# Expert pairs fed by a 128-byte gather and a 32x32 transpose on VectorE

## The chip, the cores and the metric

One core of one Trainium2 chip runs the whole program; there is no work on the other cores and no collective. The metric is the device time of one execution in microseconds. Times come as the median of several executions; the profile is of one execution, whose own time is given beside its span.

## The reference

Three layers follow one another over 4608 tokens (8 batches of 576) with 512 features, all in float32.

```
attn: phi(x) = [exp(p - max|p|), exp(-(p - max|p|))],  p = x @ w_phi
      kv = phi(k)^T v;  out = phi(q) kv / (phi(q) . sum(phi(k)) + 1e-6)      # 8 heads of 64
moe:  logits = x @ w_gate + bias[modality];  e = argmax(logits), gate = softmax(logits)[e]
      out = gate * (relu(x @ w1[e]) @ w2[e])                                  # 8 experts, 512 -> 1024 -> 512
moe2: h = x @ w_in;  s = h * softmax(h);  out = (layernorm(s) * g_ln) @ w_out # 512 -> 1024 -> 512
```

A token goes to one expert only, and which one is known only on the chip. So the middle layer must sort token rows by expert.

## The kernel before

**Attention and gating.** Eight pairs of batch and head group are worked through in 9 steps each. When a pair of batches has its last head group done, `gating` finds each token's expert, its gate and its place. GpSimd (POOL) then sends each tile of 128 token rows with one indirect DMA (line 628) into the DRAM table `xe`, whose rows have 520 floats: 512 features, the gate, the token number, and padding. There are 36 such tiles; those of the last pair of batches (4, 3 and 2 tiles) come at the end of the stage. POOL also adds up the key features (line 322).

**The experts' units.** The tokens of an expert are cut into units: unit 0 (128 rows) and unit 1 (256 rows) of the fullest expert, which start early; 16 pairs of 256 rows (units 2 to 17); one single of 128 rows (unit 18); a "quad" of four small rests; and extras under a condition that is tested once at run time (line 1412). A table in SBUF, worked out by small VectorE instructions in `slot_table` at the end of attention, tells SyncE (SP) where each unit's rows lie; SP reads four of its numbers for each unit (`slot_regs`).

**A unit's rows.** `load_x` (line 913) brings the rows of a unit into the tile `xin` with one DMA, token in the partition, and `keep_gates` (line 922) copies gate and token number from `xe` to another DRAM table. `xT` (line 898) turns the rows on TensorE in squares of 128 by 128 against the identity, eight for a pair and four for the single, into PSUM. `evac` then makes the two float32r parts of the turned rows: ScalarE copies the high part `xTh` (line 887) and VectorE subtracts it from the original for the low part `xTl` (line 888), each in pieces of 128x512. `xTh` and `xTl` have one buffer each, so they may be written for unit u+1 only when the matmuls of `mm1(u)` have read them for unit u.

**A unit's matmuls.** `mm1` (four chunks of w1) and `mm2` (four chunks of w2) run 24 matmuls for each chunk, three for each product of high and low parts (line 1074). Weight chunks are split the same way four chunks ahead (lines 925 and 926): ScalarE the high part, VectorE, or POOL in a few places (`POOL_FIRST = (1, 3)` for unit 1), the low part. Between the chunks of units 2 to 13, `prep` runs the last layer's weight conversion on VectorE in small steps (lines 997 to 1016). In `unit(u)`, after chunk `XAT` of `mm1(u)`, `next_x(u)` is called: `xT(u+1)`, `slot_regs(u+3)`, `load_x(u+2)`. From unit 14 on, blocks of the last layer run between `mm1` and `mm2`.

**What sets the order.** In attention TensorE's order is written out by hand and the other engines' orders come from the planner. From unit 2 to unit 12 the order of all engines is that of the program text; SP's queue is in program order in all of the expert stage. From unit 13 on the planner orders the compute engines of the units again. Each engine works its own queue in order, and so does SP with its DMAs.

Of the kernel before, what the change touches and what calls it, by code (L numbers as in the profile page):

```python
# [8 lines left out]
F32 = mybir.dt.float32  # L9
# [8 lines left out]
P = 128  # L18
B, H, S, D, F = 8, 8, 576, 64, 128
NTOK = B * S  # L20
DM = H * D
E = 8
# [10 lines left out]
PAD = 2 * P  # L33
CAP = NTOK + PAD
ROW = 520
YCOLS = PAD + NTOK
LAG = 8
LAGF = 2
# [152 lines left out]
    return compute  # L191


def attention(ctx, tc, c, cnt, xe, q, k, v, ld, early, m, late):
    nc = tc.nc
    V, A, G, T, SP = nc.vector, nc.scalar, nc.gpsimd, nc.tensor, nc.sync
    ldr = ctx.enter_context(tc.tile_pool(name="a_ldr", bufs=2))
# [371 lines left out]
    def gating(u, first, n):  # L569
        tiles = range(first, first + n)  # L570
        t0 = 9 * u.p2 + first
        gt = gs[0][:, 0:n] if first == 0 else gs[1][:, first - 4 : first - 4 + n]
        w = lambda nm, sh=[P, 5, E], dt=F32: gp.tile(sh, dt, name="g_" + nm)
        L = w("L")[:, :n, :]
        V.tensor_reduce(out=L, in_=gt.rearrange("p t h e -> p t e h"), axis=AX.X, op=ALU.add)
        V.tensor_tensor(out=L, in0=L, in1=c.bias[:, t0 : t0 + n, :], op=ALU.add)
        mx = w("mx", [P, 5])[:, :n]
        V.tensor_reduce(out=mx, in_=L, axis=AX.X, op=ALU.max)
        V.tensor_tensor(out=L, in0=L, in1=mx.unsqueeze(2).broadcast_to([P, n, E]), op=ALU.subtract)
        ex = w("ex")[:, :n, :]  # L580
        A.activation(ex, L, AF.Exp)
        first = w("first")[:, :n, :]
        V.scalar_tensor_tensor(
            out=first, in0=L, scalar=0.0, in1=c.rev.unsqueeze(1).broadcast_to([P, n, E]),
            op0=ALU.is_ge, op1=ALU.mult,
        )
        V.tensor_reduce(out=mx, in_=first, axis=AX.X, op=ALU.max)
        oh = w("oh", dt=BF16)[:, :n, :]
        V.tensor_tensor(
            out=oh, in0=c.rev.unsqueeze(1).broadcast_to([P, n, E]),  # L590
            in1=mx.unsqueeze(2).broadcast_to([P, n, E]), op=ALU.is_equal,
        )
# [12 lines left out]
        V.tensor_reduce(out=sm, in_=ex, axis=AX.X, op=ALU.add)
        V.tensor_scalar(out=sm, in0=sm, scalar1=1e-9, scalar2=None, op0=ALU.add)
        V.reciprocal(sm, sm)
        for part, lo, hi in ((0, 0, 4), (2, 4, 5), (1, 5, 9)):
            i0, i1 = max(lo, tiles[0]), min(hi, tiles[0] + n)
            if i0 < i1:  # L610
                G.tensor_copy(
                    xs[part][:, i0 - lo : i1 - lo, DM : DM + 1], sm[:, i0 - tiles[0] : i1 - tiles[0]].unsqueeze(2)
                )
        yield "0", 1
        base = w("base", [P, 6, E])
        V.tensor_copy(base[:, 0, :], cnt[0])
        for a in range(n):
            V.tensor_tensor(out=base[:, a + 1, :], in0=rk[:, 1, a, :], in1=base[:, a, :], op=ALU.add)
        cnt[0] = base[:, n, :]
        rkb = w("rkb")[:, :n, :]  # L620
        V.tensor_tensor(out=rkb, in0=rk[:, 0], in1=base[:, :n, :], op=ALU.add)
        V.tensor_tensor(out=rkb, in0=rkb, in1=oh, op=ALU.mult)
        dst = w("dst", [P, 5])[:, :n]
        V.tensor_reduce(out=dst, in_=rkb, axis=AX.X, op=ALU.add)
        dsti = w("dsti", [P, 5], I32)
        V.tensor_copy(dsti[:, :n], dst)
        for a, i in enumerate(tiles):
            ins = G.indirect_dma_start(
                out=xe, out_offset=bass.IndirectOffsetOnAxis(ap=dsti[:, a : a + 1], axis=0),
                in_=xt[i], in_offset=None,  # L630
            )
            tc.declare_no_dep(ins.ins, group="scat", reason="rows of distinct tokens are distinct")
            tc.add_to_no_dep_group("scat", ins.ins)

    units = [(p2, g) for p2 in range(B // 2) for g in range(2)]
    mixed = [[("k", i), ("q", i)] for i in range(9)]
# [30 lines left out]
        return U.get(len(units) - 1)  # L667

    unit(0)
    zero = w1p.tile([P, ROW], F32, name="zero")  # L670
    G.memset(zero, 0.0)
    for e in range(E):
        SP.dma_start(
            out=xe[e * CAP : e * CAP + PAD, :].rearrange("(t p) w -> p t w", p=P),
            in_=zero.unsqueeze(1).broadcast_to([P, 2, ROW]),
        )
    hl = {0: s0(*[unit(0), steps[0][1]])}
    n = len(steps)
    feats = {}
# [178 lines left out]


class Moe:  # L860
    def __init__(self, tc, c, early, ld, cv, xtp, xe, yd, gd, w1, w2, w_in, w_out, g_ln, out):
        self.tc, self.c, self.early, self.ld, self.xin, self.cv, self.xtp = tc, c, early, ld, None, cv, xtp
        self.xe, self.yd, self.gd, self.w1, self.w2, self.out = xe, yd, gd, w1, w2, out
        self.w_in, self.w_out, self.g_ln = w_in, w_out, g_ln
        self.regs, self.xs, self.raw, self.chunks, self.nsplit, self.xt = {}, {}, [], {}, 0, {}
# [24 lines left out]
    def xT(self, pool, u):  # L890
        n = self.size(u)
        hi = self.xtp.tile([P, 4, 2 * P], F32R, name="xTh")
        lo = self.xtp.tile([P, 4, 2 * P], F32R, name="xTl")
        x = self.xs.pop(u)
        for t in range(n):
            tp = pool.tile([P, 4, P], F32, name="tp")
            for k in range(4):
                self.tc.nc.tensor.transpose(tp[:, k, :], x[:, t, k * P : (k + 1) * P], self.c.ident)  # L898
            sl = slice(t * P, (t + 1) * P)
            self.evac(hi[:, :, sl], lo[:, :, sl], tp)  # L900
        self.xt[u] = (hi, lo)

    def load_x(self, u):
        SP = self.tc.nc.sync
        n = self.size(u)
        rows = self.xe[bass.ds(self.regs[u][1], n * P), :]
        if u == 0:
            t = self.hr[:, DM:].unsqueeze(1)
            self.x0 = self.hr[:, DM:]
        else:  # L910
            t = self.xin.tile([P, 2, DM], F32, name="xin") if u > 1 else self.raw[7].rearrange("p (t d) -> p t d", t=2)
            self.xs[u] = t
        SP.dma_start(out=t[:, 0:n, :], in_=rows[:, 0:DM].rearrange("(t p) w -> p t w", p=P))
        self.keep_gates(u)

    def cols(self, u):
# [1 line left out]
        return bass.ds(y0, n) if u > 1 else slice(y0, y0 + n)  # L918

    def keep_gates(self, u):  # L920
        rows = self.xe[bass.ds(self.regs[u][1], self.width(u)), :]
        self.tc.nc.sync.dma_start(out=self.gd[self.cols(u), :], in_=rows[:, DM : DM + 2])

    def split(self, src, hi, lo, eng):
        self.tc.nc.scalar.copy(hi, src)
# [538 lines left out]
        block()  # L1464


XAT = 1
ENDMAN = True
START = 14
NMAN = START - 1  # L1470
# [8 lines left out]
@with_exitstack  # L1479
def linear_attention_moe_solu(  # L1480
    ctx, tc, q, k, v, w_phi, modality_id, w_gate, modality_bias, w1, w2, w_in, w_out, g_ln, out
):
    nc = tc.nc
    xe = tc.dram_tile([E * CAP, ROW], F32, name="xe")
    yd = tc.dram_tile([DM, YCOLS], F32, name="yd")
    gd = tc.dram_tile([YCOLS, 2], F32, name="gd")
    cp = ctx.enter_context(tc.tile_pool(name="consts", bufs=1))
    fin = cp.tile([P, E], F32, name="fin")
    ld = ctx.enter_context(tc.tile_pool(name="ld", bufs=3))
    cv = ctx.enter_context(tc.tile_pool(name="cv", bufs=2))  # L1490
    xtp = ctx.enter_context(tc.tile_pool(name="xtp", bufs=1))
    with ExitStack() as c2:
        ca = c2.enter_context(tc.tile_pool(name="a_consts", bufs=1))
        c = setup_consts(nc, cp, ca, w_phi, w_gate)
        cnt = [c.rbase]
        early = Early(nc, cp, c)
        m = Moe(tc, c, early, ld, cv, xtp, xe, yd, gd, w1, w2, w_in, w_out, g_ln, out)
        attention(c2, tc, c, cnt, xe, q, k, v, ld, early, m, lambda: setup_bias(nc, c, ca, modality_id, modality_bias))
        nc.vector.tensor_copy(fin, cnt[0])
    m.tab = slot_table(ctx, tc, c, fin, early)  # L1500
    moe(ctx, m)
# [31 lines left out]
```

## Time and profile before

| | us |
|---|---|
| median of 3 executions (range) | 1341.18 (1339.69 to 1342.89) |
| the profiled execution's own time | 1338.16 |
| its span, first to last instruction | 1336.4 |

| engine | busy, us | share | instructions |
|---|---|---|---|
| TensorE matmul (PE) | 1301.7 | 97% | 9522 |
| VectorE (DVE) | 808.6 | 61% | 1571 |
| ScalarE (ACT) | 666.8 | 50% | 1254 |
| GpSimd (POOL) | 433.1 | 32% | 493 |

The busy share is an average over unlike stages: attention takes the first 437 us, the pairs run from 485 to about 935 us, the rest is the last layer. The mean granted clock of TensorE is 0.991 of full speed. Times in the rows below are microseconds from the span's start unless marked otherwise.

### The profile page before, as it was taken

To read this page: it belongs to the slowest core of one execution; us is meant where nothing else is said; L and a number is where in the kernel's file an instruction comes from. 1 tells how busy PE (TensorE), PEld (TensorE's weight loads), DVE (VectorE), ACT (ScalarE), POOL (GpSimd) and SP (SyncE) were. 2 spreads that over 40 slices of the span, in tenths; PEclk is the share of its full clock that TensorE was granted. 3 is DMA by queue.
4 is the path that set the end of the run, shared out by engine and by line. 5 is a ranking of instruction groups with operands and counts; after the bars stand their busy time and mean duration, and the time that the engine had idled before them with its cause. 6 is when DMAs were issued, how large, how long until landed. Compare 5 with 4: busy or idle time off the path is not lost.

```text
span 1336.4 us, 25467 instructions
## 1 busy us (share of the span) xinstructions
PE 1301.7 (97%) x9522; PEld 1095.8 (82%) x9522; DVE 808.6 (61%) x1571; ACT 666.8 (50%) x1254; POOL 433.1 (32%) x493
## 2 busy tenths in 40 slices
PE   8999999999988989999999999999999999999997
PEld 6676777777765889999999999898987777888885
DVE  8756766866954938888888754444433433444442
ACT  6665766666664335555555654444433343343332
POOL 6646664764763300000000323232323222322331
PEclk9998999999999989999999999999999999999998
DMA  8712321331132132223522212124334542111110
GB/s 238 206 52 88 112 88 56 112 120 48 60 117 71 66 94 72 83 72 106 187 73 72 66 47 64 40 56 150 112 87 150 174 129 85 48 40 48 40 41 24
DMA packets 123119, 120.08 MB, mean 90 GB/s; under 512 B 35664, under 2 KB 109552, under 8 KB 122992
## 3 DMA queue, kind: packets, MB, share of 16 engines
q1 hardware_dynamic: 117008, 99.30, 25.1%
q0 software_dynamic: 5824, 19.04, 3.9%
q8 instruction: 77, 1.26, 0.4%
q14 instruction: 50, 0.41, 0.1%
q10 hardware_dynamic: 160, 0.07, 0.0%
HBM read 148.32 MB, written 33.02 MB: 136 GB/s over the span
## 4 chain that ended last, share of the span: by engine, by line
PE 62%; issue 1%; ACT 0%; POOL 0%; POOLq 0%
PE tp L1074 42%; PE h L1074 15%; PE tp L1098 2%; PE tp L898 1%; PE tp L1349 1%; PE tp L1333 1%; PE tp L1280 0%; POOLq L1529 0%; ACT sq L1253 0%; ACT lnTh L887 0%; PE tp L1109 0%; ACT wab L1268 0%; POOL rs L1258 0%; PE tp L1162 0%; POOL rs L1256 0%
## 5 line engine op out<-in xcount | busy, mean ns | idle before, releaser
L322 POOL TENSOR_TENSOR es<-es,e 128x512 f32<-128x512 f32 x128 | 163.2, 1280 | 102.0 <-ACT e L278 96.2
L1074 PE MATMUL tp<-xTh,whi 128*128 128x256 f32 x432 | 122.5, 284 | 2.3 <-PEq L1412 2.3
L1074 PE MATMUL tp<-xTh,wlo 128*128 128x256 f32 x432 | 121.5, 281 | 1.2 <-DVE wlo L926 1.2
L1233 DVE TENSOR_REDUCE s_mx<-h 128x1 f32<-128x512 f32 x72 | 46.4, 686 | 125.3 <-PE h L1074 125.3
L1074 PE MATMUL tp<-xTl,whi 128*128 128x256 f32 x432 | 121.3, 281 | 0.0
L1074 PE MATMUL tp<-hTl,whi 128*128 128x256 f32 x432 | 120.7, 280 | 0.0
L1074 PE MATMUL tp<-hTh,wlo 128*128 128x256 f32 x432 | 120.7, 279 | 0.0
L1074 PE MATMUL tp<-hTh,whi 128*128 128x256 f32 x432 | 120.5, 279 | 0.0
L926 POOL TENSOR_TENSOR wlo<-ldk,whi 128x1024 fp32r<-128x1024 f32 x6 | 14.6, 2432 | 314.2 <-PE tp L1074 295.5
L271 DVE TENSOR_REDUCE m<-mm 128x4 f32<-128x512 f32 x144 | 97.1, 682 | 23.7 <-PE mm L269 23.0
L1238 ACT ACTIVATE ex<-h,s_mx,gt 128x1024 f32<-128x1024 f32 x36 | 43.4, 1207 | 135.7 <-DVE s_mx L1235 72.2
L1269 POOL DMA_INDIRECT out_dram<-wab,gt x36 | 38.6, 1071 | 221.6 <-ACT wab L1268 220.9
L259 DVE TENSOR_TENSOR lo<-tp,hi 128x512 fp32r<-128x512 f32 x72 | 49.5, 688 | 78.7 <-ACT hi L258 78.5
L267 PE MATMUL mm<-wphi_hi,hi 128*128 128x256 f32 x288 | 94.0, 327 | 1.6 <-ACT hi L258 1.6
L1074 PEld LDWEIGHTS tp<-xTh,whi 128*128 128x128 f32 x432 | 82.0, 190 | 2.8 <-ACTq L1412 2.5
L1074 PEld LDWEIGHTS tp<-xTh,wlo 128*128 128x128 f32 x432 | 81.9, 190 | 1.5 <-DVE wlo L926 1.5
L888 DVE TENSOR_TENSOR lnTl<-tp,lnTh 128x512 fp32r<-128x512 f32 x74 | 47.6, 686 | 58.2 <-ACT lnTh L887 58.2
L338 ACT ACTIVATE qp<-tp 128x512 f32<-128x512 f32 x128 | 69.5, 597 | 25.8 <-PE tp L330 23.0
L1074 PEld LDWEIGHTS tp<-xTl,whi 128*128 128x128 f32 x432 | 82.0, 190 | 0.2
L1074 PEld LDWEIGHTS tp<-hTh,whi 128*128 128x128 f32 x432 | 81.3, 188 | 0.4
L1074 PEld LDWEIGHTS tp<-hTl,whi 128*128 128x128 f32 x432 | 81.2, 188 | 0.3 <-DVE hTl L1089 0.2
L268 PE MATMUL mm<-wphi_lo,hi 128*128 128x256 f32 x288 | 81.5, 283 | 0.0
(427 smaller groups left out, 3930.7 us busy)
## 6 DMA issues: line engine op xcount, KB each, us to landing
ldk<-in_moe_w_dram SPq DMA_DIRECT2D x66, 512.0 KB
ldv<-in_moe_w_dram SPq DMA_DIRECT2D x66, 512.0 KB
ldq<-in_moe_w_dram SPq DMA_DIRECT2D x44, 512.0 KB
yd<-yo SPq DMA_DIRECT2D x36, 256.0 KB
yin<-yd SPq DMA_DIRECT2D x18, 512.0 KB
xin<-xe SPq DMA_DIRECT2D x16, 512.0 KB
ldk<-in_k_dram SPq DMA_DIRECT2D x15, 512.0 KB
ldq<-in_q_dram SPq DMA_DIRECT2D x15, 512.0 KB
```

Source lines behind the costliest of these rows:

```text
L259: V.tensor_tensor(out=lo, in0=tp, in1=hi.bitcast(F32), op=ALU.subtract)
L267: T.matmul(o, lhsT=hi[:, 2 * a + j, :], rhs=c.wphi_hi, start=(j == 0), stop=False, skip_group_check=True)
L268: T.matmul(o, lhsT=hi[:, 2 * a + j, :], rhs=c.wphi_lo, start=False, stop=False, skip_group_check=True)
L271: V.tensor_reduce(out=m, in_=pj, axis=AX.X, op=ALU.max, apply_absolute_value=True)
L322: G.tensor_tensor(out=eo, in0=eo, in1=ev[:, :, r, :], op=ALU.add)
L338: A.activation(u.qp[half][:, fh, 2 * hp : 2 * hp + 2, o : o + 2 * P], tp.rearrange("p (h r) t -> p h (r t)", r=2), AF.Exp, scale=sc,)
L888: self.tc.nc.vector.tensor_tensor(out=lo, in0=tp, in1=hi.bitcast(F32), op=ALU.subtract)
L1074: T.matmul(o, lhsT=l, rhs=r, start=first and n == 0, stop=last and n == 2, skip_group_check=True)
L1098: T.transpose(tp[:, j, :], src[:, (b0 + j) * P : (b0 + j + 1) * P], c.ident)
L1233: V.tensor_reduce(out=mx, in_=h[:, sl], axis=AX.X, op=ALU.max, negate=True)
L1238: A.activation(ex, h, AF.Exp, bias=mx, scale=g, accum_out=sm)
L1269: ins = G.indirect_dma_start(out=out, out_offset=bass.IndirectOffsetOnAxis(ap=ys.pop(i)[2].bitcast(I32), axis=0), in_=ob, in_offset=None,)
```

## The change

The row in DRAM is cut in two tables: `xe` with 512 features a row, and `xg` with 8 floats a row for gate, token number and padding. Each tile of tokens is sent with two indirect DMAs, and the regions in front of each expert's rows are cleared in both tables.

For units 2 and up, `load_x` reads the rows in runs of 32 floats (128 bytes) with four DMAs, one for each group of 32 partitions, so that feature block and token block have changed places and only the 32x32 squares are left to be turned. `xT` then turns all squares of the unit with one VectorE instruction in place, and `split` makes the high part (ScalarE, line 925 of before) and the low part (VectorE, line 926) from SBUF in one piece of 128x1024 each. Units 0 and 1 keep the old way. `XAT` goes from 1 to 3, so that `next_x` comes after the last chunk of `mm1`.

```diff
+GROW = ROW - 512
@@ gating
-            ins = G.indirect_dma_start(
-                out=xe, out_offset=bass.IndirectOffsetOnAxis(ap=dsti[:, a : a + 1], axis=0),
-                in_=xt[i], in_offset=None,
-            )
+            for n, (dst, src) in enumerate(((xe, xt[i][:, 0:DM]), (xg, xt[i][:, DM:ROW]))):
+                ins = G.indirect_dma_start(
+                    out=dst, out_offset=bass.IndirectOffsetOnAxis(ap=dsti[:, a : a + 1], axis=0),
+                    in_=src, in_offset=None,
+                )
@@ attention
     for e in range(E):
-        SP.dma_start(
-            out=xe[e * CAP : e * CAP + PAD, :].rearrange("(t p) w -> p t w", p=P),
-            in_=zero.unsqueeze(1).broadcast_to([P, 2, ROW]),
-        )
+        for dst, w in ((xe, DM), (xg, GROW)):
+            SP.dma_start(
+                out=dst[e * CAP : e * CAP + PAD, :].rearrange("(t p) w -> p t w", p=P),
+                in_=zero[:, 0:w].unsqueeze(1).broadcast_to([P, 2, w]),
+            )
@@ Moe.xT
         x = self.xs.pop(u)
+        if u > 1:
+            hi, lo = [t.rearrange("p k w -> p (k w)")[:, 0 : n * DM] for t in (hi, lo)]
+            self.tc.nc.vector.transpose(x, x)
+            self.split(x, hi, lo, self.tc.nc.vector)
+            self.xt[u] = [t.rearrange("p (k w) -> p k w", k=4) for t in (hi, lo)]
+            return
@@ Moe.load_x
+        elif u > 1:
+            t = self.xin.tile([P, 2 * DM], F32, name="xin")[:, 0 : n * DM]
+            self.xs[u] = t
+            src = rows.rearrange("(t c) (k g r) -> g c k t r", c=32, g=4, r=32)
+            for g in range(4):
+                SP.dma_start(
+                    out=t[32 * g : 32 * g + 32].rearrange("c (k t r) -> c k t r", k=4, r=32), in_=src[g]
+                )
+            self.keep_gates(u)
+            return
@@ Moe.keep_gates
-        rows = self.xe[bass.ds(self.regs[u][1], self.width(u)), :]
-        self.tc.nc.sync.dma_start(out=self.gd[self.cols(u), :], in_=rows[:, DM : DM + 2])
+        rows = self.xg[bass.ds(self.regs[u][1], self.width(u)), :]
+        self.tc.nc.sync.dma_start(out=self.gd[self.cols(u), :], in_=rows[:, 0:2])
@@
-XAT = 1
+XAT = 3
```

## Rows read from the trace of the kernel before

**Rows 1.** Page, part 5: line engine operation, count | busy, mean ns | idle, releaser.

```profile
L322 POOL TENSOR_TENSOR es<-es,e 128x512 f32<-128x512 f32 x128 | 163.2, 1280 | 102.0 <-ACT e L278 96.2
```

**Rows 2.** Chain of waits, one pair unit: start us, us, what.

```profile
586.72 0.87 PE tp L898 x8
587.59 22.49 PE tp L1074 x192
...
```

**Rows 3.** Chain of waits, last units.

```profile
...
874.62 0.87 PE tp L898 x8
...
922.14 0.44 PE tp L898 x4
...
```

**Rows 4.** Windows, one per pair unit: length, busy by engine, clock, DMA share, GB/s.

```profile
587.59:610.95 23.36, 23.36 (x203) 23.36 (x202) 18.42 (x26) 13.77 (x20) 0.00 (x0) 1.00 0.29 72
...
sum 257.75, PE 257.75 PEld 257.59 DVE 217.51 ACT 141.49 POOL 2.61; mean PE 23.43 PEld 23.42 DVE 19.77 ACT 12.86 POOL 0.24
```

**Rows 5.** Waits of VectorE, 493 to 752: us in total, times, longest.

```profile
DVE xTl L888 <- ACT xTh L887: 17.9, 10, 2.6
DVE wlo L926 <- ACT whi L925: 6.4, 11, 1.2
...
DVE wout0l L1016 <- ACT wout0h L1015: 1.6, 2, 0.8
...
```

**Rows 6.** Groups by line on VectorE, 498.9 to 712.

```profile
L926 DVE TENSOR_TENSOR wlo<-ldk,whi 128x1024 fp32r<-128x1024 f32 x21 | 25.7, 1223 | 2.8 <-ACT whi L925 2.6
...
L888 DVE TENSOR_TENSOR xTl<-tp,xTh 128x512 fp32r<-128x512 f32 x20 | 12.9, 686 | 17.0 <-ACT xTh L887 17.0
...
L1000 DVE TENSOR_SCALAR wab<-wab 128x512 int32<-128x512 int32 x14 | 5.9, 422 | 0.0
...
L1016 DVE SCALAR_TENSOR_TENSOR wout1l<-wab,gl,wout1h 128x512 fp32r<-128x512 f32 x2 | 1.5, 752 | 1.6 <-ACT wout1h L1015 1.6
```

**Rows 7.** Groups by line on ScalarE, 498.9 to 712.

```profile
L925 ACT CAST whi<-ldv 128x1024 fp32r<-128x1024 f32 x22 | 23.2, 1056 | 0.0
```

**Rows 8.** Timeline of VectorE: start, us, instruction, idle before it and releaser.

```profile
593.86 1.29 DVE L888 TENSOR_TENSOR xTl<-tp,xTh 128x512 fp32r<-128x512 f32 x2 [2.53 <-ACT xTh L887]
```

**Rows 9.** Windows early in attention, while 256-byte runs are loaded.

```profile
8.00:10.00 2.00, 1.81 (x7) 1.59 (x8) 2.00 (x15) 0.62 (x2) 0.79 (x9) 1.00 1.02 175
```

**Rows 10.** Timeline of POOL at the end of attention.

```profile
429.61 1.02 POOL L628 DMA_INDIRECT xe<-xt,g_dsti  x1 [2.28 <-DVE g_dsti L626]
430.93 0.96 POOL L628 DMA_INDIRECT xe<-xt,g_dsti  x1 [0.30 <-issue]
...
447.39 2.44 POOL L926 TENSOR_TENSOR wlo<-ldq,whi 128x1024 fp32r<-128x1024 f32 x1
449.77 2.40 POOL L926 TENSOR_TENSOR wlo<-ldk,whi 128x1024 fp32r<-128x1024 f32 x1
```

**Rows 11.** Timeline of ScalarE, unit 1.

```profile
450.24 0.60 ACT L1088 ACTIVATE hTh<-tp 128x512 fp32r<-128x512 f32 x1 [0.35 <-PE tp L1074]
```

**Rows 12.** Timeline of VectorE, the slot table.

```profile
446.74 5.47 DVE L751 TENSOR_TENSOR st_tail<-st_tail,st_mini 128x8 f32<-128x8 f32 x1
...
467.97 0.17 DVE L832 CAST st_tab<-st_res 128x5 int32<-128x5 f32 x1
```

**Rows 13.** Timeline of all engines, from the table to unit 2.

```profile
470.75 0.39 SPq L913 DMA_DIRECT2D xin<-xe  x1
...
474.85 0.11 SPq L884 DMA_DIRECT2D ldk<-in_moe_w_dram  x1
...
475.73 1.50 PE L898 MATMUL tp<-ident,xin 128*128 128x128 f32 x8 [2.81 <-DMA xin<-xe]
...
478.46 1.23 DVE L926 TENSOR_TENSOR w<-ldv,w 128x1024 fp32r<-128x1024 f32 x1
...
485.35 0.36 PE L1074 MATMUL tp<-xTh,whi 128*128 128x256 f32 x1 [2.33 <-PEq L1412]
```

**Rows 14.** Windows just after TensorE's wait for xin.

```profile
476.00:478.00 2.00, 2.00 (x13) 2.00 (x12) 1.91 (x2) 2.00 (x4) 0.00 (x0) 0.55 0.01 4
```

More of the change, by code (lines that the diff above doesn't have):

```diff
@@ L191, in setup_bias, with attention @@
     return compute
-def attention(ctx, tc, c, cnt, xe, q, k, v, ld, early, m, late):
+def attention(ctx, tc, c, cnt, xe, xg, q, k, v, ld, early, m, late):
     nc = tc.nc
@@ L627, in gating @@
         for a, i in enumerate(tiles):
-            ins = G.indirect_dma_start(
-                out=xe, out_offset=bass.IndirectOffsetOnAxis(ap=dsti[:, a : a + 1], axis=0),
-                in_=xt[i], in_offset=None,
-            )
-            tc.declare_no_dep(ins.ins, group="scat", reason="rows of distinct tokens are distinct")
-            tc.add_to_no_dep_group("scat", ins.ins)
+            for n, (dst, src) in enumerate(((xe, xt[i][:, 0:DM]), (xg, xt[i][:, DM:ROW]))):
[3 more added lines that the diff above has]
+                )
+                tc.declare_no_dep(ins.ins, group=f"scat{n}", reason="rows of distinct tokens are distinct")
+                tc.add_to_no_dep_group(f"scat{n}", ins.ins)
     units = [(p2, g) for p2 in range(B // 2) for g in range(2)]
@@ L669, in attention @@
     unit(0)
-    zero = w1p.tile([P, ROW], F32, name="zero")
+    zero = w1p.tile([P, DM], F32, name="zero")
     G.memset(zero, 0.0)
     for e in range(E):
-        SP.dma_start(
-            out=xe[e * CAP : e * CAP + PAD, :].rearrange("(t p) w -> p t w", p=P),
-            in_=zero.unsqueeze(1).broadcast_to([P, 2, ROW]),
-        )
+        for dst, w in ((xe, DM), (xg, GROW)):
[3 more added lines that the diff above has]
+            )
     hl = {0: s0(*[unit(0), steps[0][1]])}
@@ L860, with __init__ @@
 class Moe:
-    def __init__(self, tc, c, early, ld, cv, xtp, xe, yd, gd, w1, w2, w_in, w_out, g_ln, out):
+    def __init__(self, tc, c, early, ld, cv, xtp, xe, xg, yd, gd, w1, w2, w_in, w_out, g_ln, out):
         self.tc, self.c, self.early, self.ld, self.xin, self.cv, self.xtp = tc, c, early, ld, None, cv, xtp
+        self.xg = xg
         self.xe, self.yd, self.gd, self.w1, self.w2, self.out = xe, yd, gd, w1, w2, out
@@ L909, in load_x @@
             self.x0 = self.hr[:, DM:]
+        elif u > 1:
[8 more added lines that the diff above has]
+            return
         else:
-            t = self.xin.tile([P, 2, DM], F32, name="xin") if u > 1 else self.raw[7].rearrange("p (t d) -> p t d", t=2)
+            t = self.raw[7].rearrange("p (t d) -> p t d", t=2)
             self.xs[u] = t
-        SP.dma_start(out=t[:, 0:n, :], in_=rows[:, 0:DM].rearrange("(t p) w -> p t w", p=P))
+        SP.dma_start(out=t[:, 0:n, :], in_=rows.rearrange("(t p) w -> p t w", p=P))
         self.keep_gates(u)
@@ L1483, in linear_attention_moe_solu @@
     nc = tc.nc
-    xe = tc.dram_tile([E * CAP, ROW], F32, name="xe")
+    xe = tc.dram_tile([E * CAP, DM], F32, name="xe")
+    xg = tc.dram_tile([E * CAP, GROW], F32, name="xg")
     yd = tc.dram_tile([DM, YCOLS], F32, name="yd")
@@ L1496, in linear_attention_moe_solu @@
         early = Early(nc, cp, c)
-        m = Moe(tc, c, early, ld, cv, xtp, xe, yd, gd, w1, w2, w_in, w_out, g_ln, out)
-        attention(c2, tc, c, cnt, xe, q, k, v, ld, early, m, lambda: setup_bias(nc, c, ca, modality_id, modality_bias))
+        m = Moe(tc, c, early, ld, cv, xtp, xe, xg, yd, gd, w1, w2, w_in, w_out, g_ln, out)
+        attention(c2, tc, c, cnt, xe, xg, q, k, v, ld, early, m, lambda: setup_bias(nc, c, ca, modality_id, modality_bias))
         nc.vector.tensor_copy(fin, cnt[0])
```

## The prediction, made before the changed kernel was run

> **What bounds the kernel now.** I read the chain of waits first. From unit 2 to the end it is TensorE and little else: a pair unit is 22.49 us of matmuls (192 of them) and 0.87 us of eight transposes of `xin`, with nothing between [rows 2]. So in this stage what leaves TensorE leaves the time, as long as no other engine becomes the slowest. The windows, cut at the transposes, tell which that would be: over 11 pair units (493.65 to 751.40) a unit lasts 23.43 us, TensorE is busy all of it, VectorE 19.77 us [rows 4]. VectorE has 3.66 us to spare, and the waits of VectorE say what they are: 17.9 us of the 40.3 are the low part of the turned rows, waiting for its high part, which ScalarE may write only after `mm1` has let go of the one buffer [rows 5]. After about 751 us the last layer's weights are done and VectorE has room. The third view is the timeline between the stages, where TensorE waits twice: 2.81 us for the first `xin` and 2.33 us at the condition [rows 13].
>
> **What the change takes away.** The eight transposes of units 3 to 18: eleven groups at the cuts of the eleven windows, one just ahead of them, three pairs and a single after them [rows 2, 3]. That is 11 x 0.87 = 9.6 us at most in the windows, and 0.87 + 3 x 0.87 + 0.44 = 3.9 us outside, where VectorE is no limit; the second sum I take whole. Of the 9.6 less is left, as follows.
>
> **VectorE in units 3 to 13.** Out: the two low parts of 128x512, 1.29 us for the pair as they overlap [rows 8]. In: a transpose of 128x1024 that no row shows, and one low part of 128x1024 from SBUF, 1.22 us as for the weights [rows 6]. Nothing is as near to the transpose as these passes over 1024 elements of a partition: the fastest row gives 2 x 0.42 = 0.84 us, the slowest 2 x 0.75 = 1.50 us, and I take 1.22 us, the row of the same shape [rows 6]. Busy: 19.77 - 1.29 + 1.22 + 1.22 = 20.92 us.
>
> Then the waits. In the program's order transpose, high part and low part follow one another with nothing between, so VectorE stands still while ScalarE copies: 1.06 us [rows 7]. That stands in for the 1.63 us a unit (17.9 / 11) that goes. Of the other 2.0 us of idle time a unit, the last layer's 16 chunks keep their wait for ScalarE, 0.7 to 0.8 us each [rows 5], which is 1.1 us a unit; the rest may go when VectorE is late anyway, since its inputs then lie ready. A round of VectorE is 20.92 + 1.06 + 1.1 = 23.1 us at the least and 24.0 us with all waits; TensorE without the transposes needs 22.55 us. I take 23.3 us, near the low end because a late engine finds little to wait for. So VectorE, not TensorE, becomes the bound here.
>
> It starts with a lead. The last chunk of `mm1` in the unit shown ends at 587.59 + 5.6 = 593.2 us; relu on ScalarE 0.60 [rows 11], its low part 0.69, a weight split 1.22 [rows 6], a step of `prep` of about 1 us, then 1.22 + 1.06 + 1.22 us put the low part of the next rows at 600.2 us, while `mm1` of the next unit wants it at 593.2 + 11.25 = 604.4 us. The lead of about 4 us is used up before TensorE waits at all: 11 x 23.3 - 4 = 252.3 us against 257.75 us, a gain of 5.4 us. TensorE sets the floor at 11 x 22.55 = 248 us (gain 9.7). With the slow ends (1.50 us and all waits, round 24.3 us) it is 263.3 us, a loss of 5.5 us.
>
> The Trainium skill has a rule against this ("VectorE: DVE Perf Modes", Rules for kernel authors): it sends a 128x128 transpose to TensorE where PSUM will do as a destination, and its section on the three transpose paths gives VectorE 311 ns for a 128x128 bf16 tile in 32x32 blocks. Eight such tiles would be an estimate of 2.5 us; by that the round is 24.6 us and the windows lose 8.4 us. No row of the trace shows a VectorE transpose; the rows of the same shape stand at half of it.
>
> **The gather.** Each pair asks for 4096 runs of 128 bytes in four DMAs. It can be issued when the low part of the unit before is written, and is wanted a round later, less the 3.5 us from transpose to low part: some 18 us may pass. From below it takes what it takes now, 5 us from issue to use (470.75 to 475.73) [rows 13]; from above, the stretch with 256-byte runs moves 175 GB/s with all 16 DMA engines full [rows 9], 23 ns a run on each, so 4096 runs need 6 us, and 12 us if a run of half the length cost double. I take 6 to 8 us, hidden; it is late only beyond 18 us. On SP the three more DMAs cost 3 x 0.6 us a unit, which nothing waits for except at unit 2.
>
> **POOL and the start of unit 2.** A scatter costs POOL 0.96 us and a gap of 0.30 us [rows 10]. The price of a narrow one no row shows: between the gap alone and 1.27 us; as both address 128 rows I take 1.27 us. The first 27 tiles add 34 us spread over a stage in which POOL idles 96 us for ScalarE's exponentials [rows 1]: hidden, 0.5 us for what leaks (none to 3). The last nine are not. From 429.61 to 447.39 us POOL does nine scatters (11.4 us) and a few copies; nine more fill the 5.8 us of gaps and push the rest out by 5.6 us. Behind them in POOL's order stand the two low parts of unit 1's weights [rows 10], now ready at 455.4 and 457.8 us. TensorE is through its first chunk at 450.2 us [rows 11] and needs the first of them: a new wait of 5 us. After the 2.8 us wait for `xin` the granted clock was 0.55 of 2.4 GHz, so mostly the lower level [rows 14]; I add 2 us for some 4 us of that. The same path loses the 2.81 us wait, its slow clock and unit 2's transposes, some 6 us. TensorE alone comes out even.
>
> What decides is the slot table's path. One of its small VectorE instructions now lasts 5.47 us and ends with POOL's second split [rows 12]; with POOL later, this stall meets a VectorE that waits for TensorE's late chunks anyway, and I put the table (467.97) 0 to 2.3 us later. Then SP needs 1.8 us more for four DMAs ahead of the reload at 474.85 us, on which the weight splits hang. Their third ends at 479.7 us [rows 13], then about 483.8; transpose, high part, the old copy behind it on ScalarE, four transposes of `put_rows` and the 2.33 us at the condition come to 489.6 us, where unit 2 now starts at 485.35 us [rows 13]. So between 0.6 us (TensorE alone) and 4.3 us; I take 3 us.
>
> **Sum.** -5.4 (windows) - 3.9 (other units) + 3 (start of unit 2) + 0.5 (attention) = -5.8 us. The profiled execution took 1338.16 us, so 1332.4; the median of the runs shown lies 3.0 us above that execution: 1335.4 us.
>
> **Rivals.** (a) TensorE stays the bound: VectorE's round is under 22.9 us (transpose at 0.84 us, few waits) and the narrow scatters are nearly free. -9.7 - 3.9 + 0.6 = -13.0: 1328.2 us. For it speaks that much of VectorE's idle time is one wait that the new order removes; against it that three instructions in a row now depend on one another across two engines. (b) A draw: the round is 23.7 us (windows -1.0) and the start costs 4.3 us. -1.0 - 3.9 + 4.3 + 0.5 = -0.1: 1341.1 us. (c) Slower: VectorE's round passes the old unit. Place: units 3 to 13; price: eleven times whatever the round has beyond 23.43 us, less the lead of 4 us. With a round of 24.3 us and the late start: +5.5 - 3.9 + 4.3 + 0.5 = +6.4: 1347.6 us. It decides from a round of about 24.0 us. The skill's figure above would put it at +8.4 - 3.9 + 3 + 0.5, so 1349.2 us. (d) The gather is late: at 20 us, every pair waits 2 us for it, 22 us in all, near 1355 us; against it speaks the factor of two to three over the rate seen.
>
> **Chances.** The forecast 0.40, (a) 0.15, (b) 0.19, (c) 0.23, (d) 0.03. A change under 0.2% (2.7 us) can't be told from none. Faster: 0.40 + 0.15 = 0.55; the same 0.19; slower 0.26. The range takes in (a) and (c): 1327 to 1349 us; the forecast's own is 1331 to 1338.
>
> **What the new profile would show.** Right: no transposes of `xin` on TensorE; in the pair units VectorE above 95% busy or waiting for `xTh`, TensorE with short waits for VectorE that begin only after a few units, which start at 22.5 us and then last some 23.3 us; units from 14 on shorter by 0.87 us; 72 scatters of about 1 us, and a 5 us wait of TensorE near 450 us for POOL's split. Wrong: a transpose far from 1.2 us; no wait of TensorE for VectorE (then rival a); waits of VectorE for `xin` (then rival d); a start of unit 2 that moves by more than 5 us or comes earlier.

## The result, and the profile after

The changed kernel took 1347.37 us (median of 7 runs, 1345.31 to 1350.39), the kernel before on the same chip 1340.56 (7 runs, 1336.97 to 1343.45): a ratio of 1.0055, 95% interval 1.0040 to 1.0071. It is slower by some 7 us. The forecast was 1335.4 us, 5.8 us under; the time is that of rival (c), but, as the stages show, not its mechanism.

The profiled execution took 1350.39 us with a span of 1348.7 (before: 1338.16 and 1336.4), 12.3 us more span; it is the slowest of the seven, so this pair shows more than the 6.8 us between the medians. To see where, I cut both spans at the same events: the first products of unit 1, of unit 2, of unit 4 and of unit 12, the first products of the 512-column blocks that follow the pair units, a late one of those blocks, and the issue of the last scatter of the result. Windows of the kernel before (start and end, length, busy us of each engine with its count, granted clock, DMA share, GB/s):

```profile
0.00:447.10 447.10, 428.35 (x3679) 313.25 (x3679) 313.68 (x719) 275.77 (x658) 259.05 (x263) 0.99 0.34 106
447.10:485.35 38.25, 31.87 (x256) 31.28 (x254) 26.82 (x96) 15.00 (x21) 5.05 (x3) 0.96 0.10 32
485.35:534.08 48.73, 48.73 (x401) 48.57 (x402) 34.46 (x49) 23.52 (x32) 0.00 (x0) 0.96 0.35 94
534.08:721.33 187.25, 187.25 (x1603) 187.25 (x1602) 157.67 (x218) 101.31 (x140) 0.00 (x0) 1.00 0.33 101
721.33:768.12 46.79, 46.79 (x403) 46.79 (x402) 37.12 (x46) 28.52 (x39) 9.76 (x5) 1.00 0.25 69
768.12:952.22 184.10, 184.10 (x1222) 167.80 (x1221) 84.58 (x133) 84.56 (x125) 54.68 (x56) 1.00 0.23 71
952.22:1328.39 376.17, 374.59 (x1975) 300.82 (x1973) 154.26 (x315) 138.14 (x243) 103.49 (x168) 1.00 0.27 83
1328.39:1336.40 8.01, 0.00 (x0) 0.00 (x0) 0.00 (x0) 0.00 (x0) 1.07 (x1) 0.57 0.09 33
```

The same windows of the changed kernel:

```profile
0.00:450.39 450.39, 432.27 (x3678) 315.04 (x3679) 316.28 (x722) 275.90 (x658) 290.03 (x296) 0.98 0.34 105
450.39:492.93 42.54, 31.42 (x247) 30.64 (x246) 27.32 (x94) 14.89 (x20) 8.38 (x6) 0.90 0.16 36
492.93:543.48 50.55, 48.79 (x385) 47.92 (x386) 32.96 (x43) 21.26 (x28) 0.00 (x0) 0.95 0.34 72
543.48:731.33 187.85, 183.43 (x1538) 181.18 (x1537) 166.40 (x219) 100.09 (x131) 0.00 (x0) 1.00 0.42 102
731.33:780.44 49.11, 46.64 (x386) 45.49 (x385) 44.50 (x49) 30.05 (x39) 11.49 (x5) 1.00 0.36 72
780.44:961.48 181.04, 181.04 (x1194) 164.72 (x1193) 90.13 (x134) 84.08 (x122) 54.28 (x56) 1.00 0.27 73
961.48:1337.70 376.22, 374.64 (x1975) 300.85 (x1973) 154.25 (x315) 138.11 (x243) 103.41 (x167) 1.00 0.27 83
1337.70:1348.70 11.00, 0.00 (x0) 0.00 (x0) 0.00 (x0) 0.00 (x0) 1.08 (x1) 0.66 0.06 24
```

Row by row: +3.3 us up to unit 1, +4.3 to unit 2, +1.8 over units 2 and 3, +0.6 over the eight rounds of units 4 to 11, +2.3 behind them, -3.1 in the blocks, nothing in the long stage after, and +3.0 behind the last scatter. The fourth row of each is the core of the case: before, TensorE is busy all of the 187.25 us; after, its work has shrunk to 183.43 us, but the eight rounds take 187.85, 23.48 us each. TensorE now stands still for another engine. VectorE is busy 166.40 / 8 = 20.80 us a round ([rows 4] had 19.77). Its timeline in one unit, then ScalarE's row between:

```profile
562.14 1.24 DVE L901 STREAM_TRANSPOSE xin<-xin 128x1024 f32<-128x1024 f32 x1
...
564.49 1.23 DVE L946 TENSOR_TENSOR xTl<-xin,xTh 128x1024 fp32r<-128x1024 f32 x1 [1.11 <-ACT xTh L945]
```

```profile
563.41 1.05 ACT L945 CAST xTh<-xin 128x1024 fp32r<-128x1024 f32 x1 [4.78 <-DVE xin L901]
```

The transpose takes 1.24 us, and behind it VectorE waits 1.11 us for the high part, then makes the low part: 3.58 us in a row in which no weight split is made. That wait is the largest that VectorE has left (waits of VectorE, 543 to 731: us in total, times, longest); [rows 5] had 17.9 us for its predecessor over 11 units:

```profile
DVE xTl L946 <- ACT xTh L945: 10.0, 9, 1.1
DVE wlo L946 <- ACT whi L945: 3.0, 5, 0.7
```

And what TensorE waits for, 480 to 770, where before it waited for the condition alone:

```profile
PE tp L1094 <- DVE wlo L946: 4.9, 8, 0.8
PE tp L1182 <- ACT yr L1177: 4.0, 1, 4.0
PE tp L1094 <- PEq L1432: 3.5, 1, 3.5
PE tp L1094 <- DVE w L946: 1.2, 2, 0.7
```

The stretch between the attention and unit 2 in the changed kernel, against [rows 10, 12, 13]: timelines of POOL, TensorE, VectorE and SP, each in a fence of its own.

```profile
429.60 1.02 POOL L630 DMA_INDIRECT xe<-xt,g_dsti  x1 [1.81 <-DVE g_dsti L627]
430.92 0.96 POOL L630 DMA_INDIRECT xg<-xt,g_dsti  x1 [0.30 <-issue]
...
453.63 1.38 POOL L630 DMA_INDIRECT xg<-xt,g_dsti  x1 [0.30 <-issue]
455.04 2.35 POOL L946 TENSOR_TENSOR wlo<-ldq,whi 128x1024 fp32r<-128x1024 f32 x1
457.34 2.37 POOL L946 TENSOR_TENSOR wlo<-ldk,whi 128x1024 fp32r<-128x1024 f32 x1
```

```profile
457.44 0.58 PE L1094 MATMUL tp<-xTh,wlo 128*128 128x256 f32 x1 [3.69 <-POOL wlo L946]
...
488.35 1.11 PE L1182 MATMUL tp<-ident,yr 128*128 128x128 f32 x4 [3.95 <-ACT yr L1177]
492.93 0.55 PE L1094 MATMUL tp<-xTh,whi 128*128 128x256 f32 x1 [3.47 <-PEq L1432]
```

```profile
455.37 4.38 DVE L758 TENSOR_SCALAR st_room<-st_pst 128x8 f32<-128x8 f32 x1
...
470.83 0.17 DVE L835 CAST st_tab<-st_res 128x5 int32<-128x5 f32 x1
```

```profile
473.59 3.39 SPq L925 DMA_DIRECT2D xin<-xe  x4
...
480.72 0.12 SPq L888 DMA_DIRECT2D ldk<-in_moe_w_dram  x1
```

A narrow scatter costs POOL the same 0.96 + 0.30 us as a wide one, the eighteen end at 455.0 us, TensorE waits 3.69 us for POOL's first split, a VectorE instruction over 8 columns is held for 4.38 us until POOL's second split ends, the four gather DMAs take SP 3.39 us, the reload comes at 480.72 instead of 474.85 us, and unit 2 starts 7.6 us later than before. The table is 2.9 us later from the span's start; counted from unit 1's first products, which are 3.3 us later themselves, it is 0.4 us earlier (20.4 us behind them, 20.9 before).

### The profile page after: what moved, and what is told of

Read it like the earlier page. It is cut to its first block, busy times and chain, and to the rows that moved or that the text cites. A ratio compares the mean times of both kernels' runs of the same rounds, so it can differ in the third digit from the quotient of the medians.

```text
span 1348.7 us, 25433 instructions
## 1 busy us (share of the span) xinstructions
PE 1298.2 (96%) x9390; PEld 1085.8 (81%) x9390; DVE 831.8 (62%) x1572; ACT 664.4 (49%) x1238; POOL 468.7 (35%) x529
## 4 chain that ended last, share of the span: by engine, by line
PE 44%; DVE 8%; issue 4%; ACT 3%; DMA 2%; SPq 1%; POOL 0%; POOLq 0%; DVEq 0%; ACTq 0%
PE tp L1094 26%; PE h L1094 15%; DVE wlo L946 3%; PE tp L1118 2%; SPq L925 1%; DMA xin<-xe 1%; DVE hTl L1109 1%; ACT whi L945 1%; DVE xin L901 1%; ACT xTh L945 1%; DVE xTl L946 1%; DMA ex<-in_moe_w_in_dram 1%; PE tp L1369 1%; PE tp L1353 1%; DMA yin<-in_moe_w_in_dram 0%
## 5 line engine op out<-in xcount | busy, mean ns | idle before, releaser
L272 DVE TENSOR_REDUCE m<-mm 128x4 f32<-128x512 f32 x144 | 97.0, 682 | 23.4 <-PE mm L270 22.4
L270 PE MATMUL mm<-wphi_hi,lo 128*128 128x256 f32 x288 | 81.6, 283 | 0.0
```

The source lines that it names most:

```text
L270: T.matmul(o, lhsT=lo[:, 2 * a + j, :], rhs=c.wphi_hi, start=False, stop=True, skip_group_check=True)
L272: V.tensor_reduce(out=m, in_=pj, axis=AX.X, op=ALU.max, apply_absolute_value=True)
```

## Experiments

Fourteen runs in four sets, each set on one chip beside the kernel before (the first on one chip, the other three on another). In the first and the last set the kernel before took 1345.3 and 1346.0 us, in the second and third 1339.4 and 1339.5; this difference matters below, so times are compared within a set, and across sets by stages.

**First set: the suspects one by one.** e1 is the kernel before with the second table alone; against the changed kernel, the row loads and TensorE's transposes of before come back (loads not shown):

```
-            self.tc.nc.vector.transpose(x, x)
-            self.split(x, hi, lo, self.tc.nc.vector)
...
-XAT = 3
+XAT = 1
```

> The kernel before with the two DRAM tables alone (two scatters a tile); loads, turns on TensorE and XAT as before. Theory A (VectorE's round is the bound in the pair units, and the narrow scatters delay unit 1's weight splits and so the start of unit 2): pair units stay at 23.4 us, TensorE waits 3 to 4 us for POOL near 450 us, unit 2 starts some 3 to 4 us later than before; 1343 to 1345 us against 1340.6 before. Theory B (the scatters are the whole loss): 1347 us. Theory C (the 128-byte gather is the whole loss): 1340.6 us.

Measured: 1389.51 us, ratio 1.0333 (1.0312 to 1.0355). e3 takes the transpose out of the changed kernel (the rows are used unturned):

```
-            self.tc.nc.vector.transpose(x, x)
```

> The changed kernel without VectorE's transpose instruction (left out: the rows reach the matmuls unturned). Theory A: VectorE's round falls from 23.5 by 1.2 to about 22.3 us, under TensorE's 22.55, so units 3 to 13 last 22.6 us and the time is 8 to 10 us less than the changed kernel's 1347.4: about 1338 us. Theory B and C (scatters or gather): no change, 1346 to 1348 us.

Measured: 1381.96 us, ratio 1.0285 (1.0269 to 1.0301). e4 issues the transpose earlier, after the third of the four chunks of the previous unit's `mm1`; the high and low part stay after the fourth (`turn`, which holds the transpose, is not shown):

```
+            if i == XAT - 1 and u + 1 < NU:
+                m.turn(u + 1, m.xs[u + 1])
             if i == XAT:
```

> The changed kernel with the transpose issued one chunk earlier (after the third chunk of mm1) and high and low part where they are. VectorE's work is the same, only its wait of 1.1 us a unit for the high part should go, since ScalarE can copy while VectorE does the fourth chunk's parts. Theory A in its form 'the round, waits included, is the bound': round 22.4 us, units at 22.6 us, about 1338 us. In its form 'the busy time is the bound': no change, 1347 us. Theory C (late gather): the turn comes earlier, so VectorE waits for xin and it is no better, 1347 us or more.

Measured: 1381.9 us, ratio 1.0277 (1.0258 to 1.0296). e7 gives the kernel before the later place of the row work alone:

```
-XAT = 1
+XAT = 3
```

> The kernel before with XAT = 3 and nothing else. Theory A: TensorE is the bound, so moving next_x changes no unit: 1339 to 1342 us, though the wait of VectorE for xTh (1.6 us a unit) shrinks. Rival (the later place of next_x is what costs): units above 23.6 us, 1343 us or more.

Measured: 1345.22 us, ratio 0.9994 (0.9983 to 1.0005): the place alone costs nothing.

Three whole times were 40 us off every theory, and all of it lay before unit 1, in a text that these kernels share with the changed one: unit 1 starts at 498.9, 495.0 and 498.5 us instead of 450.4. Behind that point e3 and e4 did what theory A said: from unit 1 to the end of the span 883.8 us (e3) and 884.6 (e4), against 889.3 before and 898.3 changed. e1 took 892.3 us; its rounds stayed at 23.4 us as theory A had them, but unit 2 starts 38.4 us after unit 1, where it had 3 to 4 us more than the 38.3 before.

**Second set: the changed kernel again, and two repairs.** e0 is the changed kernel without an edit.

> The changed kernel once more, beside the next two on the same chip. Three experiments with the changed kernel's attention text took 35 to 45 us more than it, all of it before expert unit 1 (start of unit 1's first products at 495.0 to 498.9 us, 450.4 in the changed kernel), in stalls of PE, ACT and DVE beside POOL's rows of eight and ten scatters. Theory X (the stall comes of the doubled scatter rows, on one chip or launch more than on another, and not of what the experiments changed behind it): this run comes near e4's 1382 plus 13, 1385 to 1397, if this chip is like that one, and the kernel before stays near 1345. Theory Y (the experiments' own edits brought it about): 1347 again, as on record.

Measured: 1347.15 us, ratio 1.0058 (1.0042 to 1.0075), unit 1 at 449.0 us. So either the edits or something about that set had made the 40 us. e6 adds to e4 that unit 2 is loaded and turned as before:

```
-        if u > 1:
+        if u > 2:
             hi, lo = [t.rearrange("p k w -> p (k w)")[:, 0 : n * DM] for t in (hi, lo)]
...
-        elif u > 1:
+        elif u > 2:
...
```

> The changed kernel with the square transpose issued after the third quarter of the previous unit's first layer, and with unit 2 loaded row by row and turned by TensorE, as before. Theory A (the lost time behind the attention is VectorE's round of 23.5 us against TensorE's 22.5, and the start of unit 2): from unit 1's first products to the end 880 to 883 us (898.3 in the changed kernel, 889.3 before, 884.6 with the early transpose alone), start of unit 2's products 38 to 39 us after unit 1's (42.5 changed, 38.3 before). The whole is then 1330 to 1337 if the attention takes what it took in the changed kernel, and 1375 to 1380 if it stalls as in the first three experiments. Rival (the gather itself holds the units back): 885 or more.

Measured: 1332.72 us, ratio 0.9954 (0.9936 to 0.9972); from unit 1 to the end 882.1 us, unit 2 37.8 us after unit 1: theory A. e10 takes the two splits behind the scatters off POOL:

```
-POOL_FIRST = (1, 3)
+POOL_FIRST = ()
```

> The changed kernel with the two weight splits that POOL does behind its last row of scatters given to VectorE. Theory A (PE's wait of 3.7 us at 457.4 us for POOL's split, and the 4.4 us of a small VectorE instruction beside it, come of the 18 scatters that end at 455 us): the wait for POOL goes, two splits of 1.22 us come to VectorE; unit 2's products start 39 to 41 us after unit 1's instead of 42.5, and the whole is 1 to 4 us below the changed kernel beside it. Rival (the wait moves to VectorE, which has the gate work of the slot table there): no gain, or 1 to 2 us lost.

Measured: 1342.88 us, ratio 1.0041 (1.0024 to 1.0059), unit 2 39.5 us after unit 1. That is 4.3 us under e0, a little more than theory A had; the stretch from unit 1 to unit 2 gives 3.6 of them.

**Third set: what the 40 us were, and the repairs together.** e4b and e1b are e4 and e1 once more, e11 has the edits of e6 and e10, e12 that of e6 for unit 2 alone.

> The kernel of e4 (square transpose issued early) once more, to tell what its 1382 us was. Theory X (a chip on which the doubled scatter rows hold up the other engines during the attention; the edit is not its cause): on another chip than that run's, unit 1's first products start at 449 to 451 us, and the whole is 450 + 885 + 2, 1335 to 1339. Theory Y (the edit changes the attention): 1380 again, with unit 1 at 495 to 499 us.

Measured: 1334.41 us, ratio 0.9962 (0.9947 to 0.9976), unit 1 at 444.2 us. The same text took 1381.9 us in the first set: the edit is not the cause, as theory X had it. (The chip, which theory X blames instead, is contradicted by the last set.) Its windows for the eight rounds of units 4 to 11 (the first, and the sum), and the transpose and the low part on VectorE's timeline:

```profile
538.11:560.66 22.55, 22.55 (x194) 22.55 (x193) 21.19 (x29) 11.06 (x14) 0.00 (x0) 1.00 0.52 103
...
sum 180.23, PE 180.23 PEld 180.23 DVE 165.78 ACT 101.52 POOL 0.00; mean PE 22.53 PEld 22.53 DVE 20.72 ACT 12.69 POOL 0.00
```

```profile
574.86 1.24 DVE L916 STREAM_TRANSPOSE xin<-xin 128x1024 f32<-128x1024 f32 x1
...
580.05 1.23 DVE L951 TENSOR_TENSOR xTl<-xin,xTh 128x1024 fp32r<-128x1024 f32 x1 [0.26 <-ACT xTh L950]
```

VectorE does the same work, 20.72 us a round, and in these eight rounds TensorE never waits: 22.53 us a round instead of 23.48. Between transpose and low part now lie 4 us in which VectorE makes other splits and ScalarE's copy is done.

> The kernel of e1 once more: the kernel before with the second table alone (wide and narrow scatters, two zero fills, gates read from the narrow table), its rows loaded and turned the old way. Theory X: unit 1 at 449 to 451 us and, with its own 892 us from there to the end, 1342 to 1346: 3 to 5 us slower than before, of which 3 are the scatters in front of unit 1. Theory Y: 1389 again.

Measured: 1340.96 us, ratio 1.0011 (0.9999 to 1.0022), unit 1 at 448.4 us, and 891.8 us from there; less than theory X had, and at the edge of what can be told from nothing.

> e6 (early transpose, unit 2 the old way) with the two splits taken off POOL as in e10. Theory A: the two gains lie in different places (in front of unit 1, and behind it) and add up: 1332.7 less 3 to 5, 1327 to 1330, unit 1's products at 443 to 446 us. Rival (VectorE, with the old TensorE turn of unit 2 beside the table of slots, is full there): unit 2 starts later by as much, 1331 to 1334.

Measured: 1328.33 us, ratio 0.9911 (0.9897 to 0.9925), the best of all, inside theory A's range. In the stages 2.7 us of that gain lie behind unit 1's first products (879.4 us to the end, 882.1 in e6). That unit 1 starts 5.0 us earlier than in e6 is no work of the edit: e4b, without it, has 444.2 too. Its windows from unit 1 to unit 12, and the small VectorE instruction that took 4.38 us:

```profile
444.85:480.22 35.37, 30.17 (x256) 29.64 (x254) 23.80 (x96) 14.90 (x21) 4.16 (x4) 0.96 0.12 40
480.22:530.73 50.51, 47.81 (x384) 47.20 (x385) 35.19 (x46) 23.39 (x30) 0.00 (x0) 0.96 0.34 74
530.73:710.96 180.23, 180.23 (x1538) 180.23 (x1537) 166.12 (x219) 102.36 (x132) 0.00 (x0) 1.00 0.45 109
```

```profile
454.85 0.16 DVE L758 TENSOR_SCALAR st_room<-st_pst 128x8 f32<-128x8 f32 x1
```

Without POOL's splits beside it the instruction takes 0.16 us, and the table is ready at 462.57 instead of 470.83 us, which is 17.7 us behind unit 1's first products instead of 20.4.

> The changed kernel with unit 2 alone loaded and turned the old way, everything else as changed (transpose in its late place). Theory A: unit 2's products start 37.5 to 38.5 us after unit 1's instead of 42.5, the rounds of 23.5 us behind it stay: 1341 to 1344, 4 to 5 us under the changed kernel. Rival (what is won at unit 2's start is lost at units 3 and 4, where VectorE has no lead): 1345 to 1348.

Measured: 1343.51 us, ratio 1.0027 (1.0016 to 1.0037): unit 2 37.8 us after unit 1, the eight rounds 187.85 us as in the changed kernel. Theory A in the whole; of the 5.3 us that unit 2's start gains against e0, 1.6 are lost again in units 2 and 3, which the rival had named.

**Fourth set: the 3 us at the end, and the transpose's own price.** In all eleven profiles with two tables so far 11.0 us lay between the issue of the last scatter and the end, in the two with one table 8.0. e13 has the narrow table and its zero fills in the kernel before, nothing else; e15 adds the narrow scatters of the first 18 tiles:

```
+            if u.p2 < 2:
+                ins = G.indirect_dma_start(out=xg, ...)
```

> The kernel before with the narrow table added and zero-filled (eight DMAs of SP at the start), but nothing scattered into it and nothing read from it. Theory S (the 3 us behind the last scatter come of the number of indirect DMAs that POOL issued): 8.0 us from the last scatter's issue to the end, the whole as before, within 1 us. Theory M (they come of the second table in memory): 11.0 us, and the whole 3 us over the kernel before.

> The same with the narrow scatters of the first 18 of the 36 tiles added; the gates are read from the wide rows as before, so the narrow table is not used. Theory S, in proportion: 9.5 us from the last scatter's issue to the end; theory S with a step, 8.0 or 11.0. Theory M: 11.0. None of these scatters stands at the end of the attention, so unit 1's first products start as in the kernel before, within 1 us; the whole is 0 to 3 us over it.

Measured: 1348.44 us, ratio 1.0015 (1.0003 to 1.0027), and 1370.72 us, ratio 1.0178 (1.0154 to 1.0201). e13 has 2.4 us over the kernel before for 1 expected. The spans end at 1348.7 and 1369.9 us; the last scatter on POOL's timeline, e13 then e15:

```profile
1340.69 1.08 POOL L1273 DMA_INDIRECT out_dram<-wab,gt  x1 [4.04 <-ACT wab L1272]
```

```profile
1360.39 1.08 POOL L1280 DMA_INDIRECT out_dram<-wab,gt  x1 [4.05 <-ACT wab L1279]
```

From issue to end 8.0 us with no extra scatter, 9.5 us with 18, 11.0 us with 36: the program's end is longer by 3.0 / 36 = 83 ns for each narrow scatter that POOL issued, theory S in proportion. Whether it counts the DMAs or their 128 rows each, these runs can't tell. The whole of e15 missed its expectation by 22 us: unit 1 starts at 478.7 us, the delay of the first set again.

> The changed kernel without VectorE's square transposes (rows are used unturned, so what is computed differs). Theory A (VectorE's round was the bound): without them the round is TensorE's 22.5 us, and the whole is that of the early transpose, 1334.4, or up to 2 us less, since unit 2's start is shorter by one transpose. Rival (the transpose costs even where it is hidden, by the shared memory or by what it delays): 4 us or more under the early transpose, 1330 or less.

Measured: 1381.18 us, ratio 1.0267 (1.0250 to 1.0285), a miss for the whole: unit 1 at 495.8 us again. Only the part behind it can be read: 882.4 us from unit 1 to the end against e4's 884.6, which was delayed like it, 2.2 us less; e3, the same kernel beside e4, had 883.8, 0.8 less. So the seventeen transposes cost 1 to 2 us once they are issued early, and without them the round is the 22.53 us of theory A. In the place that the change gave them they cost 7.6 us in the eight rounds alone (187.85 us, 180.24 in e3b). From unit 1 to the end the changed kernel takes 898.3 us, 14 to 16 more, but up to 3 of these come of the difference between the sets (e4 884.6, e4b 887.4).

The stages side by side (us):

| | unit 1 at | 1 to 2 | 2 to 4 | 4 to 12 | end | ratio |
|---|---|---|---|---|---|---|
| before | 447.1 | 38.3 | 48.7 | 187.3 | 8.0 | 1 |
| e1b, two tables | 448.4 | 37.5 | 48.9 | 187.3 | 11.0 | 1.0011 |
| changed (e0) | 449.0 | 43.1 | 49.8 | 187.9 | 11.0 | 1.0058 |
| e10, splits off POOL | 444.0 | 39.5 | 50.3 | 188.0 | 11.0 | 1.0041 |
| e12, unit 2 as before | 446.8 | 37.8 | 51.4 | 187.9 | 11.0 | 1.0027 |
| e4b, transpose early | 444.2 | 44.1 | 49.8 | 180.2 | 11.0 | 0.9962 |
| e6, e4b and e12 | 449.9 | 37.8 | 50.9 | 180.2 | 11.0 | 0.9954 |
| e11, e6 and e10 | 444.9 | 35.4 | 50.5 | 180.2 | 11.0 | 0.9911 |

## Why the prediction was wrong, step by step

**Right in mechanism and size.** VectorE becomes the bound in the units: busy 20.80 us a round (predicted 20.92), transpose 1.24 us (1.22), wait for the high part 1.11 us (1.06), round 23.48 us (23.3). Moving the one instruction, with all of VectorE's work kept, brought the round to TensorE's 22.53 us (e4b): the order of VectorE's work, not its amount, made the bound. The estimate of 2.5 us, eight times the Trainium skill's figure ("VectorE: DVE Perf Modes", The three transpose paths: 311 ns for 128x128 in bf16), is not borne out here: 1.24 us. The factor of eight is what fails; the figure itself is not contradicted. The one transpose of 128x512 took 0.71 us, so 512 more elements of a partition cost 0.53 us and some 0.19 us do not grow with the size; for 128 elements that gives an estimate of 0.32 us. And the rule that the prediction cites against the change is one for whole 128x128 tiles, while here only the 32x32 squares were left to be turned. The blocks gained 3.1 us, the narrow scatter costs 1.27 us, and TensorE's new wait is for POOL's split (3.7 us for the predicted 5). The gather is hidden in units 3 to 14: VectorE waits for `xin` only in units 15 to 18, 10.4 us in all, and TensorE, busy for all of the 181.04 us of the blocks there, does not wait with it.

**The step that failed: "It starts with a lead."** From unit 2's first products to the last scatter -9.3 us were predicted (windows -5.4, other units -3.9) and +1.7 came. The lead of 4 us was to give some five rounds at 22.55 us; by the prediction's rounds units 2 and 3 would have won 1.8 us and units 4 to 11 3.3. They lost 1.8 and 0.6, and the rest won 0.7 for 4.2. There was no lead. TensorE waits for VectorE at the end of unit 2 already (0.41 us at 513.71) and then in unit 3, not after a few units:

```profile
519.52 0.38 PE L1094 MATMUL tp<-xTh,wlo 128*128 128x256 f32 x1 [0.45 <-DVE wlo L946]
...
526.27 0.39 PE L1094 MATMUL tp<-xTh,wlo 128*128 128x256 f32 x1 [0.76 <-DVE wlo L946]
```

The windows of units 2 and 3, before and changed:

```profile
485.35:510.44 25.09, 25.09 (x200) 25.09 (x201) 14.77 (x21) 9.36 (x13) 0.00 (x0) 0.93 0.43 107
510.44:534.08 23.64, 23.64 (x203) 23.48 (x202) 19.69 (x28) 14.16 (x20) 0.00 (x0) 1.00 0.28 79
```

```profile
492.93:518.67 25.74, 25.32 (x192) 25.12 (x193) 11.63 (x15) 8.70 (x11) 0.00 (x0) 0.90 0.38 79
518.67:543.48 24.81, 23.47 (x195) 22.80 (x194) 21.34 (x29) 12.56 (x18) 0.00 (x0) 1.00 0.30 65
```

I had worked the lead out from a unit in the middle of the stage before, where the splits run ahead. At the start of the changed stage they don't. In unit 2 VectorE gets only 11.63 us of work done (14.77 before), and when the first row of transpose, copy and low part comes, no splits lie ready: what TensorE waits for above are low parts of weights. Unit 3 then takes 24.81 us for the predicted 22.55. That the transpose's place makes this, the other runs show: unit 3 takes 22.48 us without the transpose (e3b) and 23.50 with the early one (e4b). The reload on which the splits hang, 5.9 us later from the span's start and 2.6 us counted from unit 1, is at most a part of it: in e12, where it is not later, unit 3 takes 23.26 us and units 4 to 7 23.3 to 23.9. What VectorE lacks in that first turn beside this was not tried. Unit 2 itself hardly waits; it is long because of the granted clock, 0.90 on average (0.93 before) and 0.50, the lower level, in its first 4 us behind two waits of 3.95 and 3.47 us.

Behind unit 11, where 4.2 us were to be won, the blocks won 3.1, but units 12 and 13 lost 2.3: in these 49.11 us VectorE is busy 44.50, and TensorE waits 2.4 us for it. That too goes with the order: with the early transpose of e4b 602.3 us pass from unit 12 to the last scatter, in the changed kernel 606.4, before 607.1.

**Start of unit 2.** +3 predicted, bounds 0.6 to 4.3; measured +4.3 from unit 1's first products (+4.8 in e0). From the span's start it is 7.6 us, beyond the 5 us that the prediction named as a sign of being wrong; 3.3 of them lie ahead of unit 1. The path was only in part the one described. The doubled scatters and POOL's late splits cost this stretch nothing by themselves: with all of them e1b takes 37.5 us and e12 37.8, against 38.3 before, and the table is not later behind unit 1 (20.3 us in e1b, 20.4 in the changed kernel, 20.9 before). TensorE does wait 3.7 us for POOL in e1b, but its 2.8 us wait for `xin` is gone there. What is longer is SP's part, from the load of `xin` to the reload (7.1 us for 4.1; I had 1.8 more), and the way from the reload to unit 2 (12.2 us for 10.5). e12, which loads and turns unit 2 as before, takes 5.3 us off. Taking the splits off POOL wins 3.6 us (e10 against e0) and 2.4 us (e11 against e6) because the table is then earlier, 17.7 us behind unit 1; on the kernel before it was not tried.

**The end of the program: a term that was missing.** +3.0 us behind the last scatter, as large as the forecast for unit 2. I took what follows the last scatter for a constant; e13 and e15 show that it grows with POOL's narrow scatters, and not because a second table is there.

**The attention.** +0.5 predicted, +3.3 in the profiled pair. Most of that is one stretch: between 426 and 433 us the granted clock was 0.53 in this execution, 0.76 in e0 and 1.00 before, with the same order of TensorE's work behind the same wait of 3.06 us. From the end of that wait to unit 1's first products it is 20.3 us in the four profiles whose clock stayed at 1.00 there (before, e4b, e10, e11) and 21.7 to 23.1 us in the five where it fell (changed, e0, e1b, e6, e12; 23.1 in the changed kernel); the first and the last set are left out. So the nine last pairs of scatters cost this stretch nothing by themselves. Up to that wait the changed kernel is 0.5 us late in the profiled pair; over the eight of these profiles with two tables it is between 0.5 us late and 3.2 us early, so the 0.5 of the prediction is neither shown nor refuted.

**The rivals.** The place of rival (c) is right, and so nearly is its price for the windows: units 2 to 13 lost 4.7 us, for its 5.5. Its reason is not: the round would have had to be 24.3 us and was 23.48, hardly over the old 23.41. The loss lies at both ends, 1.8 us in units 2 and 3 and 2.3 in units 12 and 13, with 0.6 between. The 3.0 us at the program's end are in none of the sums, so that (c) lies within 1 us of the measured median is in part luck.

## What to carry to other kernels

When an engine with slack gets an instruction whose result goes to another engine and back, cost the place in its order, not the busy time: here a transpose of 1.24 us was nearly free one chunk earlier, with other work between, and cost about 1 us a round when transpose, copy and low part stood in a row. Work a lead out at the start of the stage, from the event that starts it, not from its steady state. And count the scatters: each narrow one took 1.27 us of POOL, which by e1b's whole time (ratio 1.0011) cost next to nothing here, and 0.08 us at the program's end.

## What the runs showed of the hardware that I had not expected

**The tail grows with the indirect DMAs.** 8.0, 9.5 and 11.0 us after the last issue with 72, 90 and 108 of them.

**The same kernel, 47 us apart.** e4 took 1381.9 us in the first set and 1334.4 in the third; e1 1389.5 and 1341.0. In the first and last set instructions that wait for TensorE are released late while POOL issues scatters. ScalarE and VectorE near 170 us in e4 (POOL's ten scatters run until 174.0):

```profile
170.13 0.21 ACT L423 COPY den<-mm 128x64 f32<-128x64 f32 x1 [3.35 <-remote]
...
175.85 0.60 ACT L339 ACTIVATE qp<-tp 128x512 f32<-128x512 f32 x1 [3.64 <-remote]
```

```profile
174.40 0.69 DVE L272 TENSOR_REDUCE m<-mm 128x4 f32<-128x512 f32 x1 [8.52 <-remote]
```

It starts 7 us after TensorE's last product for it, which ended at 167.4 us. The same VectorE instruction in e4b, the same kernel, where that product ended at 162.3:

```profile
162.29 0.69 DVE L272 TENSOR_REDUCE m<-mm 128x4 f32<-128x512 f32 x1 [1.60 <-PE mm L270]
```

The profiles of those two sets name the releaser "remote" and show no landing of any indirect DMA; in the other sets both are there. The delay goes with the scatters: unit 1 starts at 455 to 459 us with 36 of them (e7, e13), at 478.7 with 54 (e15), at 495 to 499 with 72 (e1, e3, e4, e3b), against 444 to 450 in the other sets whatever their number. So a second scatter for each tile is a risk of its own: where the kernel before loses 6 us, e4 loses 47. What makes a set one kind or the other stays open; it is not the chip alone, as the second, third and last set ran on the same one. Neither the changed kernel nor e11 was run in such a set.
